# The sinks' v rows by four transfers issued from GpSimd instead of selection matmuls, in a windowed attention with a channel mix

## The chip, the cores and the metric

The kernel runs on one core of one Trainium2 chip. A core has TensorE (PE: matrix products, which read SBUF and write PSUM), VectorE (DVE), ScalarE (ACT) and GpSimd (POOL) for elementwise work, and SyncE (SP), which here only issues transfers between HBM and SBUF. The metric is the device time of one execution in microseconds (us), lower is better; the numbers given are medians of the runs.

## The reference

Attention with a sliding window of 128 positions and four "sinks" (the first four positions, which every later position sees), and after it a channel mix in the manner of RWKV. Batch 4, 8 heads, 768 positions, head width 64; the mix has 512 channels and 1024 hidden ones. All inputs are fp32.

```python
scores = q @ k.T / sqrt(64)
keep   = (pos_k < 4) | ((pos_q - pos_k >= 0) & (pos_q - pos_k < 128))
a      = softmax(where(keep, scores, -1e9))
x      = (a @ v) with the heads joined: [4, 768, 512]
x_prev = x moved down by one position, zero at the first
xk, xr = mu_k*x + (1-mu_k)*x_prev,  mu_r*x + (1-mu_r)*x_prev
out    = sigmoid(xr @ w_r) * ((relu(xk @ w_k) ** 2) @ w_v)
```

## The kernel before

**Tiling.** The 768 positions of a batch are cut into three blocks of 256, so there are 12 units u = 3b + T (batch b, block T). `prepare` casts a unit's k, q and v to bf16 and transposes k and q: units that are not in `KD` or `QD` on TensorE with an evacuation of PSUM (lines 576 and 589), the others by transposing transfers (line 562). `attend` computes the scores of a pair of heads (line 721), their exponentials on ScalarE (line 775), the products with v (line 808), and divides by the sum (lines 822 and 825). For the units 0 and 1 the mask is added to the scores as a bias, by products with an identity (line 728; `BIAS`); for the others the exponentials are multiplied by a mask on VectorE (line 789). `mix` transposes x (line 849, or by transfers for the units of `XD`), subtracts neighbouring positions (line 877) and forms xk and xr (line 888). `ffn` has the key products (line 939), ReLU and square (949, 953, 963, 967), the gate (979, 985), the value products (997, 909) and the stores. Matrix products work on bf16.

**The sinks.** Blocks with T > 0 need the four first positions of their batch as well. `sink_keys` on GpSimd copies their k columns out of the transposed k into `ksink`, a tile with 32 columns for each pair of heads, of which eight are used (four for each head, at `4*a`), and zeros elsewhere. So the scores of all sinks come out of four small products (line 696) with 32 rows for each pair, and `vsink` must hold on the same partitions the four v rows, in the columns of their own head only: row `32*c + 4*a + i` has sink i of head 2c + a. It is made in two steps: a product with `spread`, a 128 x 128 selection matrix (line 676), puts row i of the unit's v on all the rows `32*c + 4*a + i`, for all 8 heads, into a PSUM bank; then VectorE multiplies with `hmask`, which is one where the row belongs to the head, and writes `vsink` (line 680). This happens once a batch, at T = 0. The rows that belong to no sink have a zero in `vsink`, so what the scores are there does not matter. `vsink` has a last column of ones for the sums (`make_sinks`, line 470).

**Order.** Nothing in the kernel is scheduled at run time or by a planner while it is built: `P.op` collects 1052 operations, and `ORDER` is a written list of their numbers in which they are emitted; each engine's queue runs in that order. Entries below zero are fillers: products of zeros (`zeros`, line 1018) into a free bank. There are 30 of them, all in the first 163 entries. `CHOICE` names the engine of those operations that can run on several, and `SLOTS` the buffer that each takes. PSUM has four banks for everything but the scores, and two double banks for the scores. The costs and ranks that stand with the operations were used when the lists were found and have no effect on the program. Loads of k, q and v go through three fp32 buffers each, all on SyncE's queue.

**The start.** VectorE clears tiles (`fill`, `fill_later`, lines 402 to 412). GpSimd's queue is: identity (`make_ident`), `hmask`, the two biases, `spread`, three casts of unit 1, the masks, the sinks' ones and keys. All transposes on TensorE need the identity.

Of the kernel before, what the change touches and what calls it, by code (L numbers as in the profile page):

```python
# [8 lines left out]
FP32 = mybir.dt.float32  # L9
# [9 lines left out]
    92: "ACT", 93: "ACT", 94: "ACT", 95: "ACT", 97: "ACT", 100: "ACT", 102: "DVE", 105: "DVE",  # L19
    110: "DVE", 111: "DVE", 114: "ACT", 115: "DVE", 139: "POOL", 142: "POOL", 145: "POOL", 148:  # L20
    "DVE", 150: "DVE", 151: "ACT", 152: "ACT", 154: "DVE", 161: "DVE", 191: "DVE", 193: "DVE",
    194: "DVE", 197: "DVE", 199: "DVE", 200: "DVE", 203: "DVE", 204: "DVE", 213: "DVE", 230:
    "ACT", 234: "ACT", 273: "DVE", 276: "DVE", 279: "DVE", 282: "DVE", 285: "ACT", 286: "ACT",
    298: "DVE", 306: "DVE", 315: "ACT", 354: "DVE", 364: "ACT", 365: "DVE", 367: "DVE", 383:
    "ACT", 387: "ACT", 436: "DVE", 439: "DVE", 444: "DVE", 445: "DVE", 467: "ACT", 475: "ACT",
    514: "DVE", 516: "DVE", 521: "DVE", 524: "ACT", 525: "ACT", 546: "ACT", 550: "ACT", 554:
    "ACT", 558: "ACT", 595: "DVE", 598: "DVE", 603: "ACT", 604: "ACT", 606: "DVE", 634: "ACT",
    681: "DVE", 682: "DVE", 691: "DVE", 700: "ACT", 704: "ACT", 708: "ACT", 755: "DVE", 759:
    "DVE", 760: "ACT", 772: "DVE", 781: "ACT", 785: "ACT", 789: "ACT", 834: "DVE", 836: "DVE",
    837: "DVE", 853: "ACT", 856: "DVE", 857: "ACT", 860: "DVE", 861: "ACT", 904: "DVE", 906:  # L30
    "DVE", 910: "DVE", 912: "DVE", 913: "DVE", 929: "ACT", 933: "ACT", 940: "DVE", 941: "ACT",
    994: "DVE", 995: "ACT", 999: "ACT", 1003: "ACT", 1007: "ACT", 1022: "DVE", 1026: "DVE",
    1034: "DVE", 1035: "ACT",
# [152 lines left out]
def kernel(  # L186
# [14 lines left out]
    nc = tc.nc  # L201
# [873 lines left out]
```

## Time and profile before

| | us |
|---|---|
| median of 3 runs | 165.54 (165.51 to 166.27) |
| span of the profiled execution | 164.3 |
| what the median has beside that span | 1.24 |
| TensorE busy | 158.4 (96%) |
| VectorE busy | 145.4 (89%) |
| ScalarE busy | 131.2 (80%) |
| GpSimd busy | 13.5 (8%) |

The span runs from the first to the last instruction. A profiled execution is one run; its parts are compared with its own span, and the rest of the median (1.24 us) is taken as it is. "Busy" is the time in which at least one instruction of the engine runs; matmuls overlap, so TensorE can be busy without being at its peak. A row of a group gives line, engine, operation, what is written and read, and a count, then busy us and the mean ns of one, then the idle time of the engine before them and what ended it. In the timeline the first two numbers are start and duration in us, and an x with a number says how many instructions were merged. SPq is SyncE's issuing of transfers.

### The profile page before, as it was taken

The page shows a single profiled execution, that of the slowest core. Times are in us where ns is not written, and L with a number is a line of the kernel's source. Part 1 is how long each engine was busy: PE and PEld are TensorE (multiplying, and loading weights), DVE is VectorE, ACT ScalarE, POOL GpSimd, SP SyncE. Part 2 cuts the span into 40 slices and gives each one's busy share as a digit, 9 for nine tenths or more (in the row PEclk, how much of TensorE's full clock was granted, in tenths as well). Part 3 has the DMA queues.
Part 4 walks back from the last instruction along what each step waited for, and adds up shares of the span by engine and source line. Part 5 has one row for each costly group of instructions (what it writes and reads, how often), then busy time and mean ns, then how long its engine had stood idle before and what let it go on. Part 6 is the DMA issues. An engine that isn't in the chain of part 4 may idle for free.

```text
span 164.3 us, 4195 instructions
## 1 busy us (share of the span) xinstructions
PE 158.4 (96%) x1603; PEld 102.6 (62%) x1603; DVE 145.4 (89%) x381; ACT 131.2 (80%) x218; POOL 13.5 (8%) x38
## 2 busy tenths in 40 slices
PE   6999889999999999999999999999999999999992
PEld 2455568866467587577566775856575765664851
DVE  5259999999999999989999999999999999789752
ACT  3277999999999999999999999997668759163240
POOL 6409300010000000060000000000000000000000
PEclk9999999999999999999999999999999999999999
DMA  4999999999969896999999887986996955077743
GB/s 120 247 305 311 348 335 355 301 354 210 228 154 270 135 240 148 234 198 167 224 216 157 188 156 163 235 146 150 199 123 136 362 149 200 0 90 297 262 185 128
DMA packets 79042, 34.60 MB, mean 211 GB/s; under 512 B 67112, under 2 KB 73520, under 8 KB 79024
## 3 DMA queue, kind: packets, MB, share of 16 engines
q1 hardware_dynamic: 79008, 34.35, 86.3%
q8 instruction: 12, 0.20, 0.6%
q14 instruction: 6, 0.05, 0.1%
q10 hardware_dynamic: 16, 0.00, 0.0%
HBM read 24.12 MB, written 6.29 MB: 185 GB/s over the span
## 4 chain that ended last, share of the span: by engine, by line
PE 79%; ACT 8%; SPq 4%; DMA 3%; issue 2%; DVE 1%; POOL 1%; DVEq 0%; ACTq 0%; POOLq 0%
PE bank L997 23%; PE bank L939 23%; PE bank L979 12%; PE bank L808 6%; PE sc L721 6%; SPq L337 3%; DMA qs<-in_q_dram 3%; PE bank L576 2%; ACT e L775 2%; PE bank L849 2%; ACT rl L949 1%; PE bank L763 1%; ACT qt L589 1%; PE bank L909 1%; PE bank L1018 1%
## 5 line engine op out<-in xcount | busy, mean ns | idle before, releaser
L775 ACT ACTIVATE e<-sc 128x1024 bf16<-128x1024 f32 (+1 forms) x48 | 46.1, 994 | 1.8 <-PE sc L721 1.7
L939 PE MATMUL bank<-xk,wk_sb 128*128 128x256 bf16 x384 | 47.1, 273 | 0.0
L997 PE MATMUL bank<-wv_h,kk 128*128 128x512 bf16 x184 | 43.1, 379 | 0.1
L939 PEld LDWEIGHTS <-wk_sb 128*128 128x128 bf16 x384 | 36.4, 98 | 7.4 <-issue 0.4
L949 ACT ACTIVATE rl<-bank 128x512 bf16<-128x512 f32 x40 | 24.2, 625 | 8.6 <-PE bank L939 7.1
L997 PEld LDWEIGHTS <-kk 128*128 128x128 bf16 x184 | 17.1, 98 | 17.8 <-issue 0.4
L789 DVE TENSOR_TENSOR e<-e,mask 128x1024 bf16<-128x1024 bf16 (+1 forms) x40 | 25.4, 642 | 0.7 <-ACT e L775 0.5
L979 PE MATMUL bank<-wr_sb,xr 128*128 128x512 bf16 x96 | 23.7, 379 | 0.0
L888 DVE SCALAR_TENSOR_TENSOR xk<-td,mu_all,xt 128x256 bf16<-128x256 bf16 x48 | 22.4, 483 | 0.3
L888 DVE SCALAR_TENSOR_TENSOR xr<-td,mu_all,xt 128x256 bf16<-128x256 bf16 x48 | 22.1, 475 | 0.2
L967 ACT ACTIVATE kk<-rl 128x512 bf16<-128x512 bf16 x29 | 18.3, 664 | 4.2 <-DVE rl L953 4.0
L985 ACT ACTIVATE th<-bank 128x512 f32<-128x512 f32 x24 | 15.1, 646 | 5.7 <-PE bank L979 5.7
L825 DVE TENSOR_TENSOR x<-bank,rec 128x256 bf16<-128x256 f32 x48 | 19.2, 416 | 0.4
L808 PE MATMUL bank<-vb,e 128*128 128x65 bf16 x352 | 16.6, 194 | 0.0
L1006 DVE SCALAR_TENSOR_TENSOR w<-th,bank 128x512 f32<-128x512 f32 x19 | 13.0, 682 | 3.6 <-issue 1.8
L808 PEld LDWEIGHTS <-e 128*128 128x128 bf16 x352 | 13.6, 97 | 3.5
L979 PEld LDWEIGHTS <-xr 128*128 128x128 bf16 x96 | 8.8, 98 | 8.6 <-issue 0.2
L721 PE MATMUL sc<-qt,kt 64*128 64x128 bf16 (+1 forms) x256 | 13.9, 238 | 0.0
L721 PEld LDWEIGHTS <-kt 64*128 64x128 bf16 x256 | 8.9, 94 | 5.7 <-issue 3.1
L1018 PE MATMUL bank<-warm 128*128 128x512 bf16 x30 | 10.6, 484 | 1.1 <-DVE warm L1038 1.1
L877 DVE TENSOR_TENSOR td<-xt 128x512 bf16<-128x512 bf16 x24 | 10.3, 428 | 0.7 <-ACT xt L858 0.5
L589 ACT COPY qt<-bank 128x512 bf16<-128x512 bf16 x15 | 9.4, 643 | 1.0 <-PE bank L576 1.0
(74 smaller groups left out, 161.7 us busy)
## 6 DMA issues: line engine op xcount, KB each, us to landing
ks<-in_k_dram SPq DMA_DIRECT2D x24, 256.0 KB, 4.7
qs<-in_q_dram SPq DMA_DIRECT2D x24, 256.0 KB, 4.4
vs<-in_v_dram SPq DMA_DIRECT2D x24, 256.0 KB, 4.4
out_dram<-w SPq DMA_DIRECT2D x19, 256.0 KB, 2.7
w<-in_moe_w_k_dram SPq DMA_DIRECT2D x2, 1024.0 KB, 10.4
w<-in_moe_w_v_dram SPq DMA_DIRECT2D x2, 1024.0 KB, 9.3
w<-in_moe_w_r_dram SPq DMA_DIRECT2D x1, 1024.0 KB, 9.7
out_dram<-ob SPq DMA_DIRECT2D x4, 256.0 KB, 2.6
```

What stands on the lines that cost most here:

```text
L721: nc.tensor.matmul(out=sc[:, a, o0:o1], lhsT=lhs[rows], rhs=rhs[rows], start=u not in BIAS, stop=True, skip_group_check=u in BIAS)
L775: nc.scalar.activation(out=buf[ek][:, :, lo:], in_=buf[sck][:, :, lo:], func=AF.Exp, scale=scale)
L789: nc.vector.tensor_tensor(out=at, in0=at, in1=m, op=ALU.mult)
L808: nc.tensor.matmul(out=o[:, g, a, :], lhsT=e[:, a, e0:e0 + 128], rhs=rhs, start=(T == 0 and i == 0), stop=(i == len(blocks) - 1), skip_gro ...
L825: P.op("DVE", dve(256), lambda ok=ok, rk=rk, c=c: nc.vector.tensor_tensor(out=buf["x", u][:, :, 128 * c:128 * c + 128].rearrange("p g (a d ...
L888: nc.vector.scalar_tensor_tensor(out=buf[key][:, c, :], in0=buf[tk][:, i, :], scalar=mu[w][:, c:c + 1], in1=xt[:, c, t0 - 1:t0 + 255], op0 ...
L939: nc.tensor.matmul(out=ps[:, i, :], lhsT=wk_sb[:, c, 128 * f:128 * f + 128], rhs=xk[:, c, :], start=(c == 0), stop=(c == NC - 1), skip_gro ...
L949: nc.scalar.activation(out=buf[rk], in_=buf[psk].rearrange("p (i t) -> p i t", i=2), func=AF.Relu)
L967: nc.scalar.activation(out=buf["kk", u][:, 2 * f2:2 * f2 + 2, :], in_=buf[rk], func=AF.Square)
L979: nc.tensor.matmul(out=buf[psk], lhsT=buf["xr", u][:, c, 128 * g:128 * g + 128], rhs=wr_sb[:, c, :], start=(c == 0), stop=(c == NC - 1))
L985: P.op("ACT", act(512), lambda psk=psk, tk=tk: nc.scalar.activation(out=buf[tk], in_=buf[psk], func=AF.Tanh, scale=0.5), rank + 4 + g, tak ...
L997: nc.tensor.matmul(out=buf[psk], rhs=wv_h[:, f, :], lhsT=buf["kk", u][:, f, 128 * g:128 * g + 128], start=(f == 0), stop=(f == NF - 1))
```

## The change

1. `spread` and its four selection products are gone. In their place a tile `vstage` of 128 partitions x 4 batches x 64 fp32 is cleared (in `fill_later`), and four transfers issued from GpSimd load sink i of all batches and heads straight from v in HBM to the partitions `16*h + i`: 8 partitions x 4 runs of 256 bytes each, 8 KB a transfer.
2. The layout of the sinks follows: head a of a pair now has its columns at `16*a` instead of `4*a` in `ksink`, and `hmask` is one there.
3. The sinks' product takes `vstage` of the batch, broadcast over the 8 heads, times `hmask`. It can run on GpSimd or VectorE; the lists put all four on VectorE, as before. The first one stands much earlier in VectorE's queue, right behind the first two outputs of unit 0.
4. `CHOICE`, `ORDER` and `SLOTS` are new lists. No cast runs on GpSimd any more. There are 31 fillers. GpSimd's queue now starts with bias 0, the transfers for sinks 3 and 0, the identity, those for sinks 2 and 1, mask 0, `hmask`, the sinks' ones, bias 1.
5. On SyncE's queue the loads of the first units are k0, q0, first half of v0, first half of q1, second half of v0, second half of q1, k1; before, they were k0, q0, v0, first half of k1, q1, second half of k1.

The new lists are left out of the diff:

```diff
+    vstage = tile1([128, B, D], FP32, "vstage")
...
     def fill():
-        for t, value in ((ones, 1.0), (spread, 0.0), (hmask, 1.0)):
+        for t, value in ((ones, 1.0), (hmask, 1.0)):
...
     def fill_later():
-        for t in ksink + vsink:
+        for t in ksink + vsink + [vstage]:
             nc.vector.memset(t, 0.0)
...
     def make_hmask():
         for a in range(2):
             m = hmask[:, a::2, :]
-            keep(m, -4 * a, [[-32, NP], [0, D + 1]], 1, m)
-            keep(m, 3 + 4 * a, [[32, NP], [0, D + 1]], -1, m)
+            keep(m, -16 * a, [[-32, NP], [0, D + 1]], 1, m)
+            keep(m, 3 + 16 * a, [[32, NP], [0, D + 1]], -1, m)
...
-    const_op("POOL", 200.0, make_spread, ["spread"], ["ident", "ones0"], rank=-54)
...
+    for i in range(NS):
+        P.op("POOL", 1000.0, lambda i=i: nc.gpsimd.dma_start(
+            out=vstage[i::16], in_=v[:, :, i, :].rearrange("b h d -> h b d")), -50,
+            service=60.0, descs=32, reads=["stage0"], writes=[("vstage", i)])
...
-                nc.gpsimd.tensor_copy(out=kz[rows, :, 4 * a:4 * a + NS],
+                nc.gpsimd.tensor_copy(out=kz[rows, :, 16 * a:16 * a + NS],
                                       in_=first(rows))
...
-        psk = ("vsp", b)
-        P.op("PE", 220.0, lambda: nc.tensor.matmul(
-            out=buf[psk].rearrange("p (h d) -> p h d", h=H), lhsT=spread,
-            rhs=buf["vb", u][:, 0, :, 0:D], start=True, stop=True), rank + 4, lag=PE_LAG,
-            take=[("bank", psk)], hold=[("vb", u)], reads=["spread", ("vb", u, 0)], writes=[psk])
-        P.op("DVE", dve(512), lambda: nc.vector.tensor_tensor(
-            out=vsink[b % 2][:, :, 0:D], op=ALU.mult, in1=hmask[:, :, 0:D],
-            in0=buf[psk].rearrange("p (h d) -> p h d", h=H)), rank + 4, hold=[psk],
-            reads=[psk, "hmask", "sinks"], writes=[("vsink", b % 2)])
+        def sink_values(engine):
+            return lambda: engine.tensor_tensor(
+                out=vsink[b % 2][:, :, 0:D], op=ALU.mult, in1=hmask[:, :, 0:D],
+                in0=vstage[:, b, :].unsqueeze(1).to_broadcast([128, H, D]))
+
+        P.op("POOL", 1250.0, sink_values(nc.gpsimd), rank + 4, port=True,
+             alts={"POOL": (1250.0, sink_values(nc.gpsimd), True),
+                   "DVE": (dve(512), sink_values(nc.vector), True)},
+             reads=[("vstage", i) for i in range(NS)] + ["hmask", "sinks"],
+             writes=[("vsink", b % 2)])
```

More of the change, by code (lines that the diff above doesn't have):

```diff
@@ L18 @@
 CHOICE = {
[L19 to L30, printed above, removed]
@@ L31 @@
[L31 to L33 removed]
+    95: "ACT", 96: "DVE", 97: "ACT", 98: "DVE", 99: "ACT", 100: "DVE", 101: "DVE", 102: "ACT",
+    103: "DVE", 104: "DVE", 105: "ACT", 107: "ACT", 108: "DVE", 110: "ACT", 111: "ACT", 113:
+    "DVE", 114: "DVE", 116: "DVE", 117: "DVE", 118: "DVE", 120: "DVE", 141: "DVE", 143: "ACT",
@@ new lines @@
+    144: "ACT", 146: "ACT", 147: "ACT", 149: "DVE", 150: "ACT", 152: "ACT", 153: "DVE", 154:
+    "DVE", 156: "DVE", 163: "DVE", 193: "DVE", 195: "ACT", 196: "ACT", 198: "ACT", 199: "ACT",
+    201: "ACT", 202: "DVE", 204: "ACT", 205: "DVE", 206: "ACT", 208: "DVE", 215: "DVE", 223:
+    "ACT", 224: "DVE", 227: "ACT", 228: "DVE", 231: "ACT", 232: "DVE", 235: "ACT", 236: "ACT",
+    275: "DVE", 277: "DVE", 278: "ACT", 280: "ACT", 281: "DVE", 283: "ACT", 284: "DVE", 286:
+    "ACT", 287: "ACT", 288: "ACT", 290: "DVE", 292: "DVE", 299: "DVE", 307: "ACT", 308: "ACT",
@@ L34 @@
+    932: "ACT", 935: "ACT", 936: "ACT", 939: "ACT", 940: "ACT", 993: "DVE", 994: "DVE", 997:
+    "ACT", 998: "DVE", 1001: "DVE", 1002: "ACT", 1005: "ACT", 1006: "ACT", 1021: "ACT", 1022:
+    "DVE", 1025: "ACT", 1026: "DVE", 1029: "ACT", 1030: "ACT", 1033: "ACT", 1034: "DVE",
 }
@@ L390 @@
     ident = tile1([128, 128], BF16, "ident")
-    spread = tile1([128, 128], BF16, "spread")
     hmask = tile1([128, H, D + 1], BF16, "hmask")
@@ L414 @@
     const_op("DVE", 500.0, fill, ["ones0"], rank=-80)
-    const_op("DVE", 1800.0, fill_later, ["sinks0", "ones", "edges"], rank=-79)
+    const_op("DVE", 1800.0, fill_later, ["sinks0", "stage0", "ones", "edges"], rank=-79)
     def keep(out, base, pattern, multiplier, in_=ones, fill=0.0):
@@ L446, in make_bias1 @@
         window_mask(early.bitcast(BF16)[:, 384:640], warm[:, 0:128], LOW)
-    def make_spread():
-        for a in range(2):
-            nc.gpsimd.tensor_copy(
-                out=spread[0:NS, :].rearrange("p (c w) -> p c w", w=32)[:, :, 4 * a:4 * a + NS],
-                in_=ident[0:NS, 0:NS].unsqueeze(1).to_broadcast([NS, NP, NS]))
     def make_hmask():
```

18 lines of the change are left out of this document (added), and 157 rows, old and new, of tables (ORDER, SLOTS).

## The prediction

> **What bounds the kernel now.** I read the page's shares first, then the chain of waits, then the busy time of each engine in three stretches, and last the timeline of the first 20 us, since the change edits that part by hand.
>
> ```profile
> span 164.3 us, 4195 instructions
> ...
> PE 158.4 (96%) x1603; PEld 102.6 (62%) x1603; DVE 145.4 (89%) x381; ACT 131.2 (80%) x218; POOL 13.5 (8%) x38
> ...
> PE 79%; ACT 8%; SPq 4%; DMA 3%; issue 2%; DVE 1%; POOL 1%; DVEq 0%; ACTq 0%; POOLq 0%
> ```
>
> TensorE is busy for 96% of the span and carries 79% of the chain that ended last, so the plain reading is "bound by TensorE". The stretches qualify it. Their columns are busy us and instructions for PE, weight loads, DVE, ACT and POOL, then the granted clock, the DMA share and GB/s:
>
> ```profile
> 0.00:25.00 25.00, 22.48 (x227) 12.60 (x228) 17.72 (x57) 17.31 (x27) 9.86 (x32) 1.00 0.95 279
> 25.00:115.00 90.00, 89.85 (x985) 60.86 (x982) 87.18 (x230) 88.36 (x152) 3.62 (x6) 1.00 0.95 210
> 115.00:161.50 46.50, 46.11 (x401) 29.17 (x399) 40.42 (x97) 25.52 (x42) 0.00 (x0) 1.00 0.69 181
> ```
>
> From 25 to 115 us three engines are full at once: TensorE idles 0.15 us of 90, ScalarE 1.64, VectorE 2.82. After 115 us only TensorE is full, and ScalarE has 20.98 us to spare. In the first 25 us the DMA share is 0.95 while ScalarE idles 7.69 us and VectorE 7.28. A busy TensorE isn't one at its peak, so two rows of the chain and one group give its pace:
>
> ```profile
> 81.96 1.73 PE bank L997 x8
> ...
> 152.41 3.49 PE bank L939 x32
> ```
>
> ```profile
> L939 PE MATMUL bank<-xk,wk_sb 128*128 128x256 bf16 x384 | 47.1, 273 | 0.0
> ```
>
> On the chain a 512-column product takes 1.73 / 8 = 0.216 us and a 256-column one 3.49 / 32 = 0.109. All 384 of the latter would take 41.9 us at that pace; they are busy for 47.1. So 5.2 us of waiting lie inside this one "busy" group: TensorE has slack that an order can use or lose, even where it shows no idle time.
>
> **What is removed.** The four selection matmuls and what they hold:
>
> ```profile
> L676 PE MATMUL bank<-vb,spread x4: 381/382/383, 16.8 to 121.6; 128*128 128x512 bf16 x4
> ```
>
> ```profile
> 18.06 0.38 PE L576 MATMUL bank<-ident,qb 128*128 128x128 bf16 x4 [0.46 <-DVE vsink L680]
> ```
>
> ```profile
> L680 DVE TENSOR_TENSOR vsink<-bank,hmask 128x512 bf16<-128x512 f32 x4 | 2.7, 678 | 0.2 <-PE bank L676 0.2
> ```
>
> A selection is 382 ns long, but in a full pipeline it costs its columns: 0.216 us. The first one runs at 16.8 us, where TensorE idles anyway, so I count three: 3 x 0.216 = **-0.65 us** (bounds 0 and 4 x 0.382 = -1.53). Each selection also held one of the four PSUM banks until VectorE's product had read it; the second row shows TensorE waiting 0.46 us for that. The wait lies in the part where loads set the pace, so I take half: **-0.23** (bounds 0 and -0.46).
>
> **Fillers.** The order list holds 31 zero matmuls where it held 30: **+0.22** at the pace above (bounds 0 and the 0.38 of a 512-column product's whole length).
>
> **The product on VectorE.** It stays there, four times, but reads an fp32 tile in SBUF, broadcast over the heads, where it read fp32 in PSUM.
>
> ```profile
> L877 DVE TENSOR_TENSOR td<-xt 128x512 bf16<-128x512 bf16 x24 | 10.3, 428 | 0.7 <-ACT xt L858 0.5
> ```
>
> No row shows the new form. The nearest above is the old product, 678 ns; the nearest below is this subtraction, two bf16 inputs of that size in SBUF, 428 ns. One operand is still fp32, so I take 678: **0** (bound 4 x 0.25 = -1.0).
>
> **The transfers on GpSimd** are the part that can hurt. The queue becomes bias 0, two transfers, the identity, two transfers, mask 0, the head mask, the sinks' ones, bias 1. The rows that price it:
>
> ```profile
> 1.29 0.29 POOL L418 TENSOR_SCALAR_AFFINE_SELECT ident<-ones 128x128 bf16<-128x128 bf16 x1 [0.77 <-DVE ones L402]
> ...
> 1.65 0.29 POOL L418 TENSOR_SCALAR_AFFINE_SELECT ident<-ident 128x128 bf16<-128x128 bf16 x1
> ...
> 2.01 0.18 POOL L424 CAST ident<-ident 8x8 f32<-8x8 bf16 x1
> 2.05 1.04 DVE L408 MEMSET vsink<- 128x520 bf16 x2
> 2.15 1.82 POOL L418 TENSOR_SCALAR_AFFINE_SELECT hmask<-hmask 128x260 bf16<-128x260 bf16 x4
> ...
> 4.86 2.41 SPq L337 DMA_DIRECT2D ks<-in_k_dram  x1
> 4.86 0.44 DVE L543 CAST kb<-ks 128x512 bf16<-128x512 f32 x1 [1.43 <-DMA ks<-in_k_dram]
> ...
> 7.04 0.39 PE L576 MATMUL bank<-ident,kb 128*128 128x128 bf16 x4
> ...
> 8.63 0.61 SPq L337 DMA_DIRECT2D ks<-in_k_dram  x1
> ...
> 12.27 0.42 DVE L825 TENSOR_TENSOR x<-bank,rec 128x256 bf16<-128x256 f32 x1
> ...
> 15.74 0.55 POOL L470 COPY vsink<-hmask 128x8 bf16<-128x8 bf16 x2
> ...
> 16.72 1.02 POOL L418 TENSOR_SCALAR_AFFINE_SELECT mask<-ones 128x128 bf16<-128x128 bf16 x3
> ...
> 17.69 0.30 POOL L434 MEMSET mask<- 4x256 bf16 x1
> ```
>
> and VectorE's room there, in the same columns as the stretches above:
>
> ```profile
> 12.00:16.00 4.00, 3.70 (x41) 2.05 (x38) 3.71 (x12) 2.98 (x6) 3.36 (x6) 1.00 1.08 308
> ```
>
> A memset of the transfers' target comes in, 256 fp32 per partition. The vsink memsets take 1.04 / 2 = 0.52 us for 520 elements, so it takes about 0.26; it stands right behind them and delays only memsets, at a time when VectorE has no q or k to cast: 0. The first transfer waits for it, until 2.05 + 1.04 + 0.26, about 3.3 us. With p for one transfer on the queue, the two selects of the identity (0.65 us from start to end) are done at 3.3 + 2p + 0.65 = 3.95 + 2p, and its small copy (the whole block takes 0.90) at 4.2 + 2p. The first transposes, at 7.04 before, stay where they are as long as p is under 1.5. Behind the other two transfers stand mask 0 (16.72 to 17.99, 1.27), the head mask (1.82) and the sinks' ones (0.55): ready at 4.2 + 4p + 3.64 = 7.84 + 4p. VectorE's sinks product for batch 0 stands right behind the second attention output, which ended at 12.69; it waits from p = (12.69 - 7.84) / 4 = **1.21** on. Behind it on VectorE are the evacuation of the first transposes of x, a k cast of unit 1 and the mix of unit 0, so the wait would be felt.
>
> No row shows a transfer issued from GpSimd. The nearest are issues on SyncE's queue: 0.61 us free, 2.41 us when it blocks. These carry 256 KB and these four 8 KB each, so I take the free one: ready at 10.3 us, **0** (bounds 0 and the blocked one's 7.84 + 9.64 - 12.69 = +4.8).
>
> The Trainium skill speaks against this place: SBUF — State Buffer, section "SBUF: two separate sides", says that a transfer issued from GpSimd has its descriptors written by GpSimd, which is locked out while VectorE runs a two-port copy or cast. By that rule p would grow by the casts it meets. VectorE's one cast before the first transposes is the 0.44 us at 4.86, and it moves to ScalarE here; so the rule should bite little in this place, and no run here shows it yet. DMA: Bandwidth & Descriptors, section "Specifications", gives about 1 us to the first byte on this path; with p at that, as an estimate, the sinks would be ready at 11.8 us and the sum would not change.
>
> **Casts off GpSimd, and the engine of each operation.** Three casts leave GpSimd. Counting the choices of both lists: casts of k, q, v +8 on ScalarE and -5 on VectorE; squares -2/+2; ReLUs +5/-5; w_k casts -2/+2; evacuations of x -3/+3; of q -1/+1.
>
> ```profile
> L536 ACT CAST kb<-ks 128x512 bf16<-128x512 f32 x10 | 6.6, 655 | 0.0
> ...
> L536 DVE CAST kb<-ks 128x512 bf16<-128x512 f32 x6 | 2.5, 412 | 0.0
> ...
> L967 ACT ACTIVATE kk<-rl 128x512 bf16<-128x512 bf16 x29 | 18.3, 664 | 4.2 <-DVE rl L953 4.0
> ...
> L963 DVE TENSOR_TENSOR kk<-rl 128x512 bf16<-128x512 bf16 x19 | 7.7, 416 | 0.0
> ...
> L949 ACT ACTIVATE rl<-bank 128x512 bf16<-128x512 f32 x40 | 24.2, 625 | 8.6 <-PE bank L939 7.1 <-ACT kk L967 0.9 <-ACT rl L949 0.2
> ...
> L953 DVE TENSOR_SCALAR rl<-bank 128x512 bf16<-128x512 f32 x8 | 5.5, 685 | 1.5 <-PE bank L939 1.5
> ...
> L501 ACT ACTIVATE wk_sb<-w 128x1024 bf16<-128x1024 f32 x4 | 4.2, 1092 | 0.0
> ...
> L507 DVE CAST wr_sb<-w 128x1024 bf16<-128x1024 f32 x1 | 0.7, 682 | 0.0
> ...
> L858 ACT COPY xt<-bank 128x512 bf16<-128x512 bf16 x10 | 6.1, 614 | 0.0
> ...
> L858 DVE COPY xt<-bank 128x512 bf16<-128x512 bf16 x8 | 3.3, 414 | 0.2 <-PE bank L849 0.2
> ...
> L589 ACT COPY qt<-bank 128x512 bf16<-128x512 bf16 x15 | 9.4, 643 | 1.0 <-PE bank L576 1.0
> ...
> L589 DVE COPY qt<-bank 128x512 bf16<-128x512 bf16 x1 | 0.7, 678 | 0.0
> ```
>
> ScalarE: 8 x 0.655 - 2 x 0.664 + 5 x 0.625 - 2 x 1.092 - 3 x 0.614 - 0.64 = +2.4 us. VectorE: -5 x 0.412 + 2 x 0.416 - 5 x 0.685 + 2 x 0.682 + 3 x 0.414 + 0.68 = -1.4 us. Together +1.0. Four of the five ReLUs belong to units 8 to 11, where ScalarE has its 21 us to spare; the three casts fall in the first 25 us, where it has 7.7. What is left for the full middle is about nothing, so **0** (bounds: -1.4 if VectorE's relief counts, +1.0 if the whole surplus lands there). If that cover is gone, each cast costs its 0.41 to 0.66.
>
> **The order** is another one throughout. SyncE's queue now issues the first half of unit 1's q ahead of the second half of unit 0's v, and k last; between the last attention output and the last unit's key products stand nine groups of four 512-column products and eight of four 256-column ones, where there were ten and eight (11.3 us of cover for the last mix against 12.1, at the pace of the chain). I see no reason for a sign: 0, with the rivals as bounds.
>
> Sum: -0.65 - 0.23 + 0.22 = -0.66 us on a span of 164.3, so 163.6. The median of the runs shown, 165.54, lies 1.24 above that span; with the same around it the forecast is **164.9 us**.
>
> **Rivals.** *The sinks' product waits on GpSimd.* The place is VectorE's queue at about 12.7 us, the price 4 us for each us by which p passes 1.21. For: all three steps (transfers, masks, ones) run on one engine in order, and VectorE has only 4.00 - 3.71 = 0.29 us idle between 12 and 16 us to give. Against: four transfers of 32 short rows are small work. At p = 1.8 the wait is 2.3 us: 164.9 + 2.3 = 167.2; it makes the kernel slower than before from p = 1.4 on. *The order takes back hidden slack.* The 5.2 us inside the key products, and as much again elsewhere, say there is room; a third of the 5.2 is 1.7: 163.2. Against: the three engines are 97% full for 90 us. *The selection was hidden.* It ran beside full VectorE and ScalarE, which set the pace, and nothing is won: 165.5. *The surplus lands in the middle*: +1.0 there: 166.5.
>
> **Chances.** Small gain 0.42 (own range 164.2 to 165.6), hidden slack 0.22, GpSimd wait 0.17, nothing 0.12, surplus 0.07. With 0.5% (0.83 us) as what a measurement of this kernel can tell from no change, 164.7 and 166.4 are the borders: faster 0.17 + 0.22 = 0.39; same 0.25 + 0.12 + 0.02 = 0.39; slower 0.17 + 0.05 = 0.22. The range that leaves about 2 in 10 out is 163.0 to 167.2.
>
> **What would show it.** Right: no instruction on the old selection line, VectorE's product near 0.68 us, four GpSimd issues under 1.2 us each, the sinks' ones done before 12.7 us, first scores at about 9.5 us, and PE busy lower by about 0.7. Wrong: idle time of VectorE before the first sinks product put down to GpSimd or a transfer; the first transposes after 7.5 us; ScalarE idle in the middle, or VectorE's share there under 95%, with the time longer.

## The result, and the profile after

The changed kernel took 166.99 us in the median (166.21 to 167.59), beside 165.84 (165.51 to 166.34) for the kernel before on the same chip: a ratio of 1.0057, interval 1.0032 to 1.0082. Measured once more, later, it took 166.62 beside 166.34: 1.0014, interval 0.9988 to 1.0039. (A ratio isn't exactly the quotient of the two medians beside it.) The forecast was 164.9 us, a small gain. It is a small loss, or at best nothing. Four runs at a lower granted clock (two of `act_mu` with 184 and 230 us, the slower of which is the one with its profile, and two of the kernel before with 204) are left out of every mean and ratio below.

From the page of the kernel after:

```profile
span 164.7 us, 4201 instructions
...
PE 157.6 (96%) x1600; PEld 101.7 (62%) x1600; DVE 143.4 (87%) x379; ACT 132.5 (80%) x223; POOL 11.4 (7%) x37
...
PE 84%; DVE 5%; POOL 4%; issue 2%; ACT 2%; POOLq 0%; DVEq 0%; ACTq 0%
```

TensorE has 0.8 us less to do, VectorE 2.0 less, ScalarE 1.3 more: the work has moved as the diff says. But the span is 0.4 us longer, and 4% of the chain (6.6 us) now lies on GpSimd, which had 1%. The busy time by stretch, in the prediction's columns:

```profile
0.00:25.00 25.00, 21.49 (x218) 11.73 (x218) 16.95 (x55) 17.18 (x28) 9.12 (x31) 1.00 0.99 279
25.00:115.00 90.00, 89.63 (x973) 60.60 (x968) 87.94 (x231) 86.28 (x147) 2.23 (x6) 1.00 1.04 212
115.00:161.50 46.50, 46.50 (x417) 29.37 (x415) 38.09 (x95) 29.07 (x50) 0.00 (x0) 1.00 0.59 173
```

In the middle and the last stretch TensorE is as full as it was. In the first it is busy for 21.49 us where it was for 22.48. So the first 25 us come next, line by line. The timeline of the kernel before, with the first two groups of scores of a pair of heads, the load of one of the mix's two vectors on ScalarE's queue, and the first key products of the channel mix:

```profile
0.81 0.55 ACTq L374 DMA_DIRECT2D ob<-in_moe_mu_r_dram  x1
...
9.54 0.50 PE L721 MATMUL sc<-qt,kt 64*128 64x256 bf16 x8
...
12.42 0.50 PE L721 MATMUL sc<-qt,kt 64*128 64x256 bf16 x8
...
23.98 1.05 PE L939 MATMUL bank<-xk,wk_sb 128*128 128x256 bf16 x8
```

The same points of the kernel after, with GpSimd's transfers and VectorE's first cast of q:

```profile
3.02 0.27 DVE L421 MEMSET vstage<- 128x256 f32 x1
3.59 1.23 POOL L491 DMA_DIRECT2D vstage<-in_v_dram  x2 [1.40 <-DVE vstage L421]
5.69 1.09 POOL L491 DMA_DIRECT2D vstage<-in_v_dram  x2
6.64 0.26 ACTq L386 DMA_DIRECT2D ob<-in_moe_mu_r_dram  x1
7.79 0.44 POOL L431 TENSOR_SCALAR_AFFINE_SELECT hmask<-hmask 128x260 bf16<-128x260 bf16 x1
7.80 0.71 DVE L553 CAST qb<-qs 128x512 bf16<-128x512 f32 x1 [4.17 <-DMA qs<-in_q_dram]
...
9.64 0.51 PE L732 MATMUL sc<-qt,kt 64*128 64x256 bf16 x8
11.54 0.19 PE L496 MATMUL bank<-ident,ob 8*128 8x8 f32 x1 [1.07 <-POOL ksink L680]
...
13.87 0.51 PE L732 MATMUL sc<-qt,kt 64*128 64x256 bf16 x8
25.85 1.04 PE L950 MATMUL bank<-xk,wk_sb 128*128 128x256 bf16 x8
```

The load of mu_r is issued at 6.64 us and not at 0.81. The small product that spreads it (L496) makes TensorE stand for 1.07 us at 11.54. The profile puts that down to GpSimd's copy of the sinks' keys, which this product doesn't read; the experiments name the load. The second scores come 1.45 us later than before, the first key products 1.87 later. Part of the 1.87 is work moved forward, as the groups of both stretches up to those key products show; of before, up to 23.98 us:

```profile
L721 PE MATMUL sc<-qt,kt 64*128 64x128 bf16 (+1 forms) x40 | 2.2, 239 | 0.0
L576 PE MATMUL bank<-ident,kb 128*128 128x128 bf16 x20 | 1.9, 220 | 0.0
```

and of after, up to 25.85 us:

```profile
L732 PE MATMUL sc<-qt,kt 64*128 64x128 bf16 (+1 forms) x52 | 2.8, 238 | 0.0
L586 PE MATMUL bank<-ident,kb 128*128 128x128 bf16 x24 | 2.2, 220 | 0.1
```

That is 0.6 + 0.3 = 0.9 us more of scores and transposes. TensorE's idle time up to the same point is 23.98 - 21.46 = 2.5 us before and 25.85 - 22.34 = 3.5 after, so about 1.0 us is lost. That is the size of the stop in this profile, but the other waits there have changed too (0.50, 0.46 and 0.30 us before; 0.4 and 0.2 after, beside the stop), so what the stop itself costs has to come from a run without it. From the first key products to the end of the span it is 164.3 - 23.98 = 140.3 us before and 164.7 - 25.85 = 138.9 after: 1.4 less, of which 0.9 is that moved work and 0.5 a real gain. So inside the span of these two profiles: -0.5 and +1.0.

The other part lies outside it. A run's time minus its own span ("outside" from here on) is 1.87 us for the kernel before (1.82 to 1.92 over all runs below) and 2.33 for the kernel after (2.27 to 2.44 in its first six runs). In twelve later runs of the kernel after ten had 2.23 to 2.46, but two had 1.95 and 2.03, which stays open. The trace doesn't tell how much of the outside lies ahead of the span and how much behind it. The transfers of the kernel after behind the end of its span, from 164 to 169 us:

```profile
DMA packets 1, 0.01 MB, mean 2 GB/s; under 512 B 0, under 2 KB 0, under 8 KB 0
...
q14 instruction: 1, 0.01, 0.6%
```

One fetch of instructions, one packet of 8 KB, 2.2 us after the last instruction. The kernel before has as many fetches on this queue within its span, six, but none behind it.

### The profile page after: what moved, and what is told of

The parts are those of the page before. It is cut to its first block, busy times and chain, and to the rows that moved or that the text cites. A ratio compares the mean times of both kernels' runs of the same rounds, so it can differ in the third digit from the quotient of the medians.

```text
span 164.7 us, 4201 instructions
## 1 busy us (share of the span) xinstructions
PE 157.6 (96%) x1600; PEld 101.7 (62%) x1600; DVE 143.4 (87%) x379; ACT 132.5 (80%) x223; POOL 11.4 (7%) x37
## 4 chain that ended last, share of the span: by engine, by line
PE 84%; DVE 5%; POOL 4%; issue 2%; ACT 2%; POOLq 0%; DVEq 0%; ACTq 0%
PE bank L1008 24%; PE bank L950 24%; PE bank L990 13%; PE bank L819 7%; PE sc L732 6%; PE bank L860 2%; PE bank L586 2%; PE bank L774 2%; PE bank L1029 1%; POOL vstage L491 1%; POOL hmask L431 1%; PE bank L920 1%; PE sc L739 1%; PE bank L707 1%; DVE x L836 1%
## 5 line engine op out<-in xcount | busy, mean ns | idle before, releaser
L786 ACT ACTIVATE e<-sc 128x1024 bf16<-128x1024 f32 (+1 forms) x48 | 45.1, 975 | 2.6 <-PE sc L732 2.6
L1008 PE MATMUL bank<-wv_h,kk 128*128 128x512 bf16 x184 | 44.7, 379 | 0.0
L960 ACT ACTIVATE rl<-bank 128x512 bf16<-128x512 f32 x45 | 26.5, 607 | 16.5 <-PE bank L950 9.7
L899 DVE SCALAR_TENSOR_TENSOR xk<-td,mu_all,xt 128x256 bf16<-128x256 bf16 x48 | 21.8, 478 | 0.1
L836 DVE TENSOR_TENSOR x<-bank,rec 128x256 bf16<-128x256 f32 x48 | 19.7, 419 | 0.4
L978 ACT ACTIVATE kk<-rl 128x512 bf16<-128x512 bf16 x27 | 16.6, 648 | 0.1
L819 PE MATMUL bank<-vb,e 128*128 128x65 bf16 x352 | 16.1, 194 | 0.2 <-ACT e L786 0.2
L833 DVE RECIPROCAL rec<-bank 128x4 f32<-128x4 f32 x48 | 7.8, 175 | 3.8 <-PE bank L819 3.1
L974 DVE TENSOR_TENSOR kk<-rl 128x512 bf16<-128x512 bf16 x21 | 8.5, 416 | 2.8 <-ACT rl L960 2.8
```

Of the source, the lines that this page charges most:

```text
L786: nc.scalar.activation(out=buf[ek][:, :, lo:], in_=buf[sck][:, :, lo:], func=AF.Exp, scale=scale)
L819: nc.tensor.matmul(out=o[:, g, a, :], lhsT=e[:, a, e0:e0 + 128], rhs=rhs, start=(T == 0 and i == 0), stop=(i == len(blocks) - 1), skip_gro ...
L836: P.op("DVE", dve(256), lambda ok=ok, rk=rk, c=c: nc.vector.tensor_tensor(out=buf["x", u][:, :, 128 * c:128 * c + 128].rearrange("p g (a d ...
L899: nc.vector.scalar_tensor_tensor(out=buf[key][:, c, :], in0=buf[tk][:, i, :], scalar=mu[w][:, c:c + 1], in1=xt[:, c, t0 - 1:t0 + 255], op0 ...
L960: nc.scalar.activation(out=buf[rk], in_=buf[psk].rearrange("p (i t) -> p i t", i=2), func=AF.Relu)
L978: nc.scalar.activation(out=buf["kk", u][:, 2 * f2:2 * f2 + 2, :], in_=buf[rk], func=AF.Square)
```

## The experiments

All results in one table. Time, span and outside are means over the runs in us; the ratio to the kernel before, on the same chip, has its 95% interval. "Late fetch" is how long after the end of the span the profiled run moves its last 8 KB of instructions. The groups of runs were taken on different chips, so spans of two groups are best compared by their distance from the kernel before in the same group.

| kernel | time | span | outside | ratio | late fetch |
|---|---|---|---|---|---|
| before (three groups of runs) | 166.2 to 166.3 | 164.4 to 164.5 | 1.87 | | none |
| after, first | 166.90 | 164.57 | 2.33 | 1.0057 [1.0032, 1.0082] | 2.2 |
| after_again | 166.60 | 164.32 | 2.29 | 1.0014 [0.9988, 1.0039] | 2.2 |
| unused | 166.81 | 164.72 | 2.08 | 1.0033 [1.0015, 1.0051] | 1.45 |
| old_order | 166.06 | 163.97 | 2.09 | 0.9993 [0.9972, 1.0014] | 1.75 |
| old_order_act | 166.27 | 164.28 | 1.98 | 0.9998 [0.9977, 1.0019] | none |
| new_sel | 172.72 | 170.62 | 2.10 | 1.0387 [1.0344, 1.043] | none |
| mu_early | 166.00 | 163.68 | 2.32 | 0.9989 [0.9974, 1.0004] | 2.15 |
| v_by_act | 165.63 | 163.84 | 1.79 | 0.9962 [0.9949, 0.9976] | none |
| act_mu | 165.73 | 163.92 | 1.81 | 0.9965 [0.994, 0.999] | not read |
| act_front | 166.34 | 164.54 | 1.80 | 1.0002 [0.9979, 1.0025] | none |
| act_late | 165.85 | 164.03 | 1.81 | 0.9957 [0.9936, 0.9977] | none |
| after_late | 165.79 | 164.00 | 1.79 | 0.9963 [0.994, 0.9987] | none |
| unused_front | 167.40 | 165.34 | 2.05 | 1.0057 [1.0029, 1.0084] | 1.5 |
| after_pad8 | 166.59 | 164.73 | 1.85 | 1.0021 [1.0002, 1.0041] | 0.65 |
| after_pad40 | 166.28 | 164.48 | 1.79 | 1.0016 [0.9999, 1.0032] | none |
| before_pad8 | 166.32 | 164.62 | 1.71 | 1.0016 [0.9997, 1.0035] | 0.3 |

In the last group the kernel before had 166.08 and 164.22.

### The selection matmuls, with the old order

`unused` is the kernel before with the four transfers added behind `spread`, into a tile that nothing reads:

```diff
+        for i in range(NS):
+            nc.gpsimd.dma_start(out=vstage[i::16], in_=v[:, :, i, :].rearrange("b h d -> h b d"))
```

> The kernel before, with the four GpSimd transfers added behind the selection matrix on GpSimd's queue, into a tile that nothing reads; nothing else is changed. Theory Q (a kernel that issues any transfer from GpSimd pays about 1.1 us outside the span): span about 164.3 as before, time minus span about 2.3 instead of 1.24, time up by about 1.1. Rival S (what lies around the span has nothing to do with it, the change lost its time inside the span by a late start): time minus span as in the runs of the kernel before, time the same as before.

`old_order` is the change with the lists of before: the sinks' v rows come by the transfers, put where `spread` was made, the selection products are taken out of the list, and all else stands as it stood. The operations have other numbers then; the transfers are 89 to 92:

```diff
-    131, 135, 128, 153, 6, 86, 8, 9, 142, 148, 143, 91, 154, 155, 158, 156, -1, 132, 133, 157,
+    137, 130, 155, 6, 92, 89, 91, 90, 8, 9, 144, 150, 145, 94, 156, 157, 160, 158, -1, 134, 135,
```

> The changed kernel with the order, choices and buffers of before: the selection products are left out of the old list, the four GpSimd transfers stand where the selection matrix was made, three casts are on GpSimd again. If the removed products are worth what was predicted, the span is 0.4 to 0.9 shorter than that of before. Theory Q: time minus span 2.3, so the time is 0.2 to 0.7 above before. Rival S: time minus span as before, time 0.4 to 0.9 below before.

GpSimd's timeline in the two, `unused` and then `old_order`:

```profile
5.69 2.29 POOL L457 DMA_DIRECT2D vstage<-in_v_dram  x4
```

```profile
5.64 2.29 POOL L476 DMA_DIRECT2D vstage<-in_v_dram  x4
```

Same transfers, same place, the same outside (2.08 and 2.09). The span is 0.75 us shorter in `old_order`; the prediction had 0.65 + 0.23 = 0.88. But the selection, its bank and the making of `spread` aren't all that differs, since against the kernel before the gain is only 0.4: `unused` has a span 0.36 longer than before. The profiles show where. The unit's q is cast by GpSimd when its load has come, and TensorE waits for that cast; in the kernel before, in `unused`, and then a later wait in `old_order`:

```profile
13.56 0.40 PE L576 MATMUL bank<-ident,qb 128*128 128x128 bf16 x4 [0.30 <-POOL qb L543]
```

```profile
14.16 0.40 PE L580 MATMUL bank<-ident,qb 128*128 128x128 bf16 x4 [0.74 <-POOL qb L547]
```

```profile
18.54 0.38 PE L845 MATMUL bank<-ident,x 128*128 128x128 bf16 x4 [0.63 <-DVE x L821]
```

In `unused` the cast starts at 13.25 us and not at 12.64, and the first key products come 0.60 us later (24.58 for 23.98). In `old_order`, with the same transfers, it starts at 12.54, so the transfers alone don't explain the later load. From the first key products to the end of the span it is 140.3 us in the profiles of before, `unused` and `unused_front` (140.7 in `before_pad8`), and 139.8 in those of `old_order` and `old_order_act`: about 0.5 us is what three selections less are worth there. Ahead of that point nothing is won: `old_order` has its first key products at 24.13, and in place of the wait of 0.46 us for the selection's bank stands one of 0.63 for VectorE's x.

`old_order_act` is `old_order` with the transfers on ScalarE's queue at the very start and `vstage` cleared first:

```diff
-        P.op("POOL", 1000.0, lambda i=i: nc.gpsimd.dma_start(
+        P.op("ACT", 600.0, lambda i=i: nc.scalar.dma_start(
```

> The order of before without the selection products, the four transfers on ScalarE's queue at the start. If the four GpSimd transfers cost what the kernel with the unused ones showed (0.36 inside the span, 0.21 outside), and ScalarE's queue costs nothing: span 163.6, time minus span 1.87, ratio 0.995 to 0.997. Rival: the transfers cost the same 0.36 inside whatever queue issues them, since they share the DMA engines with the loads: span 164.0, ratio about 0.998.

It is 0.3 us of span slower and 0.1 outside faster than `old_order`, which their intervals don't tell apart. With the old order no difference between the queues is seen.

`new_sel` goes the other way: the new lists, but with `spread` and four selection products put back ahead of VectorE's products, each in a bank that the lists leave free there.

```diff
-                in0=vstage[:, b, :].unsqueeze(1).to_broadcast([128, H, D]))
+                in0=chosen[b].rearrange("p (h d) -> p h d", h=H))
+        def select():
+            chosen[b] = P.pools["bank"][(1, 3, 1, 3)[b]]
+            nc.tensor.matmul(out=chosen[b].rearrange("p (h d) -> p h d", h=H), lhsT=spread,
+                             rhs=buf["vb", u][:, 0, :, 0:D], start=True, stop=True)
```

> The order of the changed kernel with the selection matrix and its four products put back (each into a bank that is free at that place, a few entries ahead of VectorE's product), no transfers for the sinks; the late load of the mixing weights stays. If removing the selection is worth in the new order what it is in the old (0.75 us of span): span 0.7 above that of the kernel with the transfers on ScalarE's queue, 164.5, and time minus span 1.8. Rival: the new order hides it, span 163.8 to 164.0.

It lost 3.9%, and that is no price of a selection. TensorE's waits in it (what waited, for whom, us in all, times, longest):

```profile
PE bank L965 <- DVE vsink L694: 2.0, 1, 2.0
...
PE bank L700 <- ACT es L729: 0.9, 1, 0.9
PE bank L700 <- DVE qt L607: 0.8, 1, 0.8
...
PE bank L875 <- DVE vsink L694: 0.6, 1, 0.6
PE bank L700 <- ACT xt L884: 0.6, 1, 0.6
```

The selection (L700) waits three times for a bank, and twice a later product waits until VectorE's sinks product has read it. In an order that wasn't made for it a selection ties TensorE to VectorE's queue, and costs about a microsecond each. As a measure of what the change removes, this run is inconclusive.

### The late load

`mu_early` is the kernel after with the second of the two small loads (operation 78) issued right behind the first, as it was before:

```diff
+ORDER.remove(78)
+ORDER.insert(ORDER.index(77) + 1, 78)
```

> The changed kernel with the second load of the mixing weights issued right behind the first at the start, instead of behind ScalarE's first evacuation (6.64 us). Theory M (TensorE's stop of 1.07 us at 10.5 us, and the second scores 1.45 us later than before, come from that load landing late): the stop is gone, second scores before 13.0 us, span 0.5 to 1.0 shorter. Rival: loads and ScalarE set the pace up to 25 us, the span changes by less than 0.3. Time minus span as in the changed kernel under both.

TensorE's timeline in it:

```profile
9.64 0.51 PE L737 MATMUL sc<-qt,kt 64*128 64x256 bf16 x8
10.40 0.22 PE L501 MATMUL bank<-ident,ob 8*128 8x8 f32 x1
...
12.77 0.50 PE L737 MATMUL sc<-qt,kt 64*128 64x256 bf16 x8
...
24.74 1.04 PE L955 MATMUL bank<-xk,wk_sb 128*128 128x256 bf16 x8
```

The stop is gone. The second scores and the first key products come 1.1 us earlier than in the kernel after, and the mean span is 0.6 to 0.9 us shorter. From the first key products to the end it is 163.7 - 24.74 = 139.0 us, against 138.9: here what the first 25 us lose arrives at the end undiminished. The outside stays at 2.32. The mean span is 0.68 us below that of the kernel before on the same chip, close to the -0.66 of the prediction's sum.

The stop isn't always as long. Three more profiles have the same start with the late load, `after_again`, `after_pad8` and `after_pad40` (the last two are described below and differ from the kernel after only from 11.7 us on):

```profile
11.37 0.20 PE L496 MATMUL bank<-ident,ob 8*128 8x8 f32 x1 [0.90 <-POOL ksink L680]
```

```profile
10.69 0.20 PE L499 MATMUL bank<-ident,ob 8*128 8x8 f32 x1 [0.23 <-POOL ob L432]
```

```profile
10.93 0.20 PE L499 MATMUL bank<-ident,ob 8*128 8x8 f32 x1 [0.47 <-POOL ksink L683]
```

The releaser that the profile names changes, but the stop follows the load: its last packet (on queue q10, which here carries only the two small loads) moves at 10.16 us in the kernel after and at 9.98, 9.29 and 9.80 in these three, and the product begins 1.1 to 1.4 us later in each. So the late load stops TensorE for 0.2 to 1.1 us from run to run, and 1.07 is the longest of the four. The first key products of these three come at 25.69, 25.00 and 25.24 us, behind the 24.74 of `mu_early` by about as much as they stop.

### Which queue, and where on it

`v_by_act` is the kernel after with the four transfers issued from ScalarE right behind the first small load; `vstage` is the first thing that VectorE clears.

```diff
-        for t, value in ((ones, 1.0), (hmask, 1.0)):
+        for t, value in ((vstage, 0.0), (ones, 1.0), (hmask, 1.0)):
...
-        P.op("POOL", 1000.0, lambda i=i: nc.gpsimd.dma_start(
+        P.op("ACT", 600.0, lambda i=i: nc.scalar.dma_start(
```

> The changed kernel with the four transfers issued from ScalarE's queue at the very start instead of GpSimd's, their target cleared first; order otherwise as changed. Theory Q: time minus span back to about 1.24, so about 1.1 less time than the changed kernel at an equal span. Rival S: time minus span stays at 2.3; the span moves by less than 0.5 either way.

It beats both kernels, the one before by 0.4%, the one after by 0.6% (165.63 / 166.60, on two chips): 0.5 us less span than before, and 1.79 outside. Its timeline also names the load that the kernel after waits for:

```profile
7.50 0.43 DVE L559 CAST qb<-qs 128x512 bf16<-128x512 f32 x1 [3.88 <-DMA qs<-in_q_dram]
...
9.06 0.51 PE L738 MATMUL sc<-qt,kt 64*128 64x256 bf16 x8
10.63 0.19 PE L502 MATMUL bank<-ident,ob 8*128 8x8 f32 x1 [0.74 <-DMA ob<-in_moe_mu_r_dram]
...
25.20 1.05 PE L956 MATMUL bank<-xk,wk_sb 128*128 128x256 bf16 x8
```

`after_again` is the kernel after itself, beside the next three.

> The changed kernel unaltered, beside the kernels of this study: time minus span about 2.3 (before: 1.87), span 0.1 to 0.4 above that of before, time 0.5 to 0.9 above.

Its span isn't longer than that of the kernel before (164.32 beside 164.47); the outside is, by 0.42. In the mean the kernel after lay 0.26 us above the kernel before here, and 1.01 in the first comparison: that is how far two of them can differ.

`act_mu` joins the edits of `v_by_act` and `mu_early`:

```diff
+for i in (89, 90, 91, 92):
+    ORDER.remove(i)
+    ORDER.insert(ORDER.index(77) + 1, i)
+ORDER.remove(78)
+ORDER.insert(ORDER.index(77) + 1, 78)
...
-        P.op("POOL", 1000.0, lambda i=i: nc.gpsimd.dma_start(
+        P.op("ACT", 600.0, lambda i=i: nc.scalar.dma_start(
```

> The changed kernel with both cures: the four transfers on ScalarE's queue at the start, and the second load of the mixing weights right behind the first. If the two causes are separate and add (0.5 us outside the span and 0.7 inside from the first, 0.9 inside from the second, less what both cure): span 162.9 to 163.5, time minus span 1.8, ratio to before 0.990 to 0.995. Rival: both only free the same 1 us at the start, which loads bound then; span 163.8 as with the transfers alone, ratio 0.996.

The cures don't add: 165.73 beside 165.63. Its spans lie in two groups, near 163.5 and near 164.5, so a part of its runs does reach what the sum would give; what decides that is open.

Up to here the outside looked like a price of issuing from GpSimd. The next four runs test that. `act_front` and `act_late` are `v_by_act` with four more transfers from GpSimd, into a spare tile that nothing reads: right behind bias 0, or behind the mask.

```diff
+    vspare = tile1([128, B, D], FP32, "vspare")
...
+        for i in range(NS):
+            nc.gpsimd.dma_start(out=vspare[i::16], in_=v[:, :, i, :].rearrange("b h d -> h b d"))
```

> The kernel with the sinks' transfers on ScalarE's queue, plus four GpSimd transfers of the same rows into a tile that nothing reads, at the front of GpSimd's queue (behind bias 0, ahead of the identity), where the changed kernel has two. Theory G (what lies around the span grows by what GpSimd issues, more so at the front): time minus span 2.2 to 2.4 instead of 1.79. Rival K (it differs from kernel to kernel for another reason; the kernel with the selection put back had 2.10 with no GpSimd transfer): 1.8 to 2.0. Inside the span: the identity comes at about 5.5 us, still ahead of the first transposes, so plus 0 to 0.4 from the transfers sharing the DMA engines.

> The same with the four unused GpSimd transfers behind the masks, at about 10 us. Theory G: time minus span about 2.0, as the unused and the old-order kernels gained 0.21 over the kernel before. Rival K: 1.8, no difference to the kernel without them. Inside the span: equal to the kernel without them, or up to 0.4 longer if the transfers hinder the loads.

`after_late` is the kernel after with its own four transfers behind bias 1, at the end of what GpSimd does first:

```diff
+for i in (89, 90, 91, 92):
+    ORDER.remove(i)
+    ORDER.insert(ORDER.index(84) + 1, i)
```

> The changed kernel with its four GpSimd transfers moved behind bias 1 on GpSimd's queue, so that identity, masks and ones come 2.3 us earlier and the transfers land at about 12 us. If the early place on GpSimd's queue is what makes the difference to ScalarE's queue: time minus span 2.0, and VectorE's first sinks product may wait for the landing, which is then 0.5 to 1 us longer in the span. Rival: the place is without effect, time minus span 2.3, span 164.3.

`unused_front` is `unused` with the transfers ahead of the identity, first of all:

```diff
     def make_ident():
+        for i in range(NS):
+            nc.gpsimd.dma_start(out=vstage[i::16], in_=v[:, :, i, :].rearrange("b h d -> h b d"))
```

> The kernel before with four unused GpSimd transfers at the very front of GpSimd's queue, ahead of the identity; nothing else changed. Theory G: time minus span 2.2 to 2.4 instead of 1.87 (2.08 with the transfers at 5.7 us). Rival K: 1.9 to 2.1, no matter where they stand. Inside the span: the identity comes at about 4.5 us, still in time, so about the 0.36 of the other unused kernel.

All four issue from GpSimd, and three of them have 1.80, 1.81 and 1.79 outside: it isn't the issue. What the place costs inside the span is seen too. `unused_front` holds the identity up and adds 0.9 us of span. `after_late` takes 0.3 to 0.6 us off the span of the kernel after and ends 0.4% below the kernel before. Its timeline:

```profile
6.68 2.38 POOL L497 DMA_DIRECT2D vstage<-in_v_dram  x4
...
7.45 0.43 DVE L559 CAST qb<-qs 128x512 bf16<-128x512 f32 x1 [3.81 <-DMA qs<-in_q_dram]
...
9.01 0.51 PE L738 MATMUL sc<-qt,kt 64*128 64x256 bf16 x8
10.76 0.20 PE L502 MATMUL bank<-ident,ob 8*128 8x8 f32 x1 [0.93 <-POOL mask L437]
...
25.07 1.04 PE L956 MATMUL bank<-xk,wk_sb 128*128 128x256 bf16 x8
```

The first scores come at 9.01 and not at 9.64: q is there 0.35 us earlier, and its cast takes 0.43 us and not 0.71. The stop for mu_r is still there.

### The fetch behind the end

The kernels with the largest outside turned out to have an 8 KB instruction fetch behind their last instruction (the table's last column). The kernel after and `after_late` differ in GpSimd's order alone. So the last three runs change only the length of GpSimd's program: eight or forty one-column memsets behind the mask, where GpSimd is idle.

```diff
+        for i in range(8):
+            nc.gpsimd.memset(spare, 0.0)
```

> The kernel after with eight one-column memsets more on GpSimd behind the mask, where it has nothing else to do; all else as it is. Open is why the kernel after spends 2.3 us outside its span, where the one with its transfers issued a little later spends 1.8: the trace of the one has an instruction fetch of 8 KB behind the end of the span, that of the other has none. Theory F (the fetch is one of GpSimd's program, and where that program ends decides whether it falls behind the end): with a longer program the late fetch is gone or has moved forward; span 164.3 to 164.6, outside 1.8, time 166.2 to 166.4, ratio 0.997 to 1.001. Rival (the late fetch does not hang on the length of GpSimd's program): it stays, outside 2.3, time 166.7 to 166.9, ratio 1.002 to 1.005.

> The same with forty such memsets. Theory F: outside 1.8 without a late fetch or, if forty reach the next block, again 2.1 to 2.3 with one; the outside part and the late fetch go together in either case. Rival: outside 2.3 with the late fetch, as in the kernel after without them.

> The kernel before with the same eight memsets. Theory F: a longer program of GpSimd brings the late fetch into this kernel too; outside 2.05 to 2.1 instead of 1.87, span as before (164.4), time 166.45 to 166.55, ratio 1.0015 to 1.002. Rival: no late fetch, outside 1.87, ratio 1.000.

Transfers behind the end of the span in `after_pad8`, where the packet comes 0.65 us after the end, and in `before_pad8`, where it comes 0.3 us after it:

```profile
q14 instruction: 1, 0.01, 0.6%
```

```profile
q14 instruction: 1, 0.01, 0.7%
```

The queues of `after_pad40` over the whole run, with a seventh fetch and none behind the end:

```profile
q14 instruction: 7, 0.06, 0.1%
```

The length of GpSimd's program does decide where that fetch falls: eight memsets move it from 2.2 us behind the end to 0.65, forty bring it in among the others, and eight bring one into the kernel before, as expected. And the outside moves with it: 2.3 to 1.85 to 1.79. But half of theory F falls: in `before_pad8` the outside does not grow to 2.05, it shrinks to 1.71. Not that there is a late fetch counts, but how late. In the order of the table's last column, 0.3, 0.65, 1.45, 1.5, 1.75, 2.15 and 2.2 us go with 1.71, 1.85, 2.08, 2.05, 2.09, 2.32 and 2.29 to 2.33. Without one it is 1.79 to 1.87 in six kernels, but also 1.98 and 2.10 in `old_order_act` and `new_sel`, so the fetch isn't all that counts there. So what the runs show is that the length and order of GpSimd's program move both the fetch and the outside; that the end waits for the fetch fits most of these numbers, but no run shows the wait itself, since the trace has no instruction behind the span.

The 0.45 us less outside didn't make `after_pad8` faster: its span came out longer, 164.73. In its profile the first key products come 0.85 us earlier than in that of the kernel after, but the rest takes 139.5 us and not 138.9. `before_pad8`, too, has 0.4 us more span. In its profile 0.24 us of it is there at the first key products (24.22 for 23.98), with loads that are late before the memsets run at about 15 us, and the rest comes behind them. So starts and ends of such kernels differ by a few tenths from profile to profile, and why is open.

## Why the prediction was wrong, step by step

**Selection and bank, -0.88.** Right in kind, too large in size. Behind the first key products 0.5 us was won, in the profiles of both orders, for the 0.65 forecast. The 0.23 for the bank isn't seen: in the old order another wait took its place (0.63 us for VectorE's x). The 0.75 between the mean spans of `unused` and `old_order` holds a later load as well.

**Product on VectorE, 0.** Right. From the view of the tile `vsink` in the kernel after, with minimum, median and maximum in ns:

```profile
L686 DVE TENSOR_TENSOR vsink<-vstage,hmask x4: 684/689/691, 14.3 to 124.0; 128x512 bf16<-128x512 f32 x4
```

689 ns beside 678, and the first stands at 14.3 us, behind no wait. So almost every sign that the prediction gave for being right was seen, from the first scores at 9.64 us to the 0.8 us less of TensorE's busy time; what was lost lay where it had named no sign.

**Transfers on GpSimd, 0 with p = 0.61.** The size was right: 1.23 / 2 = 0.62 and 2.29 / 4 = 0.57 us each. The rival that stood on it (VectorE's product waits) didn't happen; the sinks' ones were done at 10.2 us, forecast 10.3. But I had looked for the loss only at that product. What stands behind the transfers on GpSimd's queue is the head mask, and its first select, at 7.79 us, falls on VectorE's cast of q. In five runs of kernels with that sequence (after, after_again, mu_early, after_pad8, after_pad40) the cast starts between 7.64 and 7.99 us and ends at 8.50 or 8.51 in each, 0.27 us after the end of that select (7.79 + 0.44); where the head mask was made earlier it takes 0.43. In `act_front` the cast meets another select of the head mask, and ends 0.28 us after that one (7.94 for 7.23 + 0.43). Two more rows, of `mu_early` and `after_pad40`:

```profile
7.64 0.87 DVE L558 CAST qb<-qs 128x512 bf16<-128x512 f32 x1 [4.01 <-DMA qs<-in_q_dram]
```

```profile
7.99 0.51 DVE L556 CAST qb<-qs 128x512 bf16<-128x512 f32 x1 [4.37 <-DMA qs<-in_q_dram]
```

The Trainium skill, SBUF — State Buffer, section "SBUF: two separate sides", calls the ports that VectorE and GpSimd share an exclusive lock, where the loser waits for the other's whole instruction. The fixed end agrees with that. In `after_again`, `mu_early` and `after_pad8` the cast starts 0.11 to 0.15 us ahead of the select, while a memset of GpSimd still runs (7.53 to 7.83 in `mu_early`); which of GpSimd's two instructions held it no run separates. The other way of the rule, which the prediction weighed, was not seen: beside that cast `after_late` issued its four in 2.38 us, as against 2.29. Inside the span, then, the place on GpSimd's queue wasn't free: the first scores come at 9.64 us, and at 9.01 and 9.06 in `after_late` and `v_by_act`.

**Casts and engine choices, 0.** TensorE's share of the middle stretch is unchanged (89.63 of 90 us, before 89.85), and ScalarE has less to do there, not more (86.28 us, before 88.36); its surplus lies behind 115 us (29.07, before 25.52), where the prediction had put it. In all it is 1.3 us where the counting gave 2.4, and VectorE's relief is 2.0 where it gave 1.4. Of the signs for being wrong one shows a little: ScalarE idles 3.7 us of the middle stretch, before 1.6. No run tests the choices alone, nor the 0.22 for the filler.

**The order, 0: the step that failed inside the span.** I compared the loads of SyncE's queue and the groups at the end, and didn't go through ScalarE's queue, where one small load had moved behind its first work. It cost 1.07 us of TensorE's time at 11.54 us in the profile of the kernel after, and 0.23 to 0.90 in three others with that start. A load of 2 KB isn't early because it is small: issued at 6.64 us, it let TensorE go on at 11.54, 4.9 us later (3.9 to 4.2 in the three others). Taking the stop out gave 1.1 us at the first key products and a span 0.68 below before (`mu_early`). With the stop of the profiled run -0.66 + 1.0 = +0.3 is near the 0.4 by which the profiled span grew. But the -0.66 isn't shown to be made of the terms it was summed from: `v_by_act` gets -0.52 with the load still late, and both edits together (`act_mu`) give -0.55, so the two aren't separate losses that add.

**"The same around it", 1.24: the step that failed outside.** The figure itself was wrong, since it took the span of one run from the median of others; runs with both give 1.87. That is an error of 0.63 in the forecast, but not in the difference of the kernels. And it isn't a constant: 2.33 in the kernel after, +0.46, and with GpSimd's program reordered or longer it falls back to 1.79 to 1.85. With 1.87 and the span as forecast it would have been 165.5.

Together: 163.6 + 1.0 + 2.3 = 166.9, what the first runs had (166.6 in the second); with the shortest stop, 0.2, it would be 166.1. The sum is made afterwards from one profile's stop, so its closeness to 166.9 is partly luck. Of the rivals, none named either mechanism; 166.99 lay within the range, but for reasons that aren't in it.

## What to carry to other kernels

After a new order, go through every queue for the place of every load, the smallest too, and ask who stops for it: here one load of 2 KB could give back all that four matmuls had saved. Where 0.3% matters, take each run's time and span together, and don't treat the difference as a constant: the length and order of an idle engine's program moved it by half a microsecond. And an engine that is 7% busy can still set the start: put its slow work behind what the first matmuls need, and away from the casts they need.

## What the runs showed of the hardware that was not expected

- Time outside the span was 1.71 to 2.33 us for kernels with the same stores at the end, and went with the moment of an 8 KB instruction fetch, 0.3 to 2.2 us behind the last instruction (two kernels without such a fetch had 1.98 and 2.10).
- Eight one-column memsets on an idle GpSimd moved that fetch by 1.55 us (2.2 to 0.65).
- VectorE's cast of 512 columns, 0.43 us alone, ended 0.27 to 0.28 us after the end of the GpSimd select that it met, in six profiles, whenever it had begun.
- One load of 2 KB, issued at about 7 us among the big ones, let its reader go on 3.9 to 4.9 us later in four profiles of the same start, and the stop that this made was 0.23 to 1.07 us.
